# Another hand-written order of the same pieces, up to the middle of the first feed-forward layer

## The chip, the cores and the metric

The kernel runs on one core of one Trainium2 chip. The metric is the device time of the core in microseconds (us). It is given as the median of three runs of the kernel before; one further execution was profiled, and all rows below come from that one.

## What is computed

Local attention with block summaries, then two feed-forward layers, all in float32 at the interface (weights of the layers come as float64):

```python
scores_l = scale * (q @ k.T)            # batch 2, 8 heads, 768 positions, head size 64
scores_l = where(|i - j| < 16, scores_l, -1e9)
scores_s = scale * (q @ k_block_max.T) + log(32)     # 24 blocks of 32 keys
a = softmax(concat(scores_l, scores_s))
x = a @ concat(v, v_block_mean)         # heads side by side: 2 x 768 x 512
h = relu(x @ w_in)                      # 512 -> 1024
x = (h * sigmoid(conv3(h, conv_w))) @ w_out          # 1024 -> 512
x = x + relu(layernorm(x) * g_ln @ w_ch1) @ w_ch2    # 512 -> 2048 -> 512
```

## The kernel before

**Pieces and order.** The kernel first describes its work as 1932 pieces (`plan.op`), each with a name, the engines that may do it and what it must follow. The string ORDER lists them: `583V` is piece 583 on VectorE. The letters are P (TensorE), V (VectorE), A (ScalarE), G (GpSimd) and S (SP, which issues nearly all DMAs). `Plan.arrange` reads the list, and `Plan.trace` emits the pieces in that order. Each engine runs its own pieces strictly in the order of the list, and waits at a piece whose inputs or buffers are not ready; nothing behind it on that engine overtakes it.

**Stages.** For each batch the keys, queries and values come in from HBM in chunks; TensorE transposes keys (pieces kt, kb) and queries (qt), lines 374 and 367. Attention then works on units of 128 rows (64 queries of each of two windows, for four heads of one parity); two units make a group of 128 positions. Unit u has a mask product M*u* (line 479), which fills the score bank, a transpose of its probabilities P*u* (line 586) and VectorE's, ScalarE's and GpSimd's softmax between them (lines 545, 557, 565, 576). Group j, with units 2j and 2j+1, has one score product S*j* (line 487) and one value product T*j* (line 503), the **value group** of this text:

```python
for h_ in range(2):
    vv = vw[j % 3][0:NK, h_, :].rearrange("p (h e) -> p h e", h=4)
    for p in range(4):
        for a in range(2):
            T.matmul(av[...], vv[:, p, s_], ps[a][:, p, 64 * h_:64 * h_ + 64], start=True, stop=True)
```

There are 16 matmuls in a value group and 32 in the trace, since a float32 product goes twice. The value tile `vw` (three buffers) has 120 rows: 24 block means and 96 local positions. Its first half `h_ = 0` and its second half are loaded by two DMAs, piece lv*j* (line 621). The block means come once for each buffer and batch, piece vs*j* for j of 0, 1, 2 and 6, 7, 8, on VectorE or as a DMA on SP:

```python
if e == "S":
    nc.sync.dma_start(out=t[0:NB], in_=src)       # L634
else:
    on[e].tensor_copy(t[0:NB], src)               # L636
wt = [VSUM[b]] + old
LVS[i] = plan.op(f"vs{i}", (("S", 60), ("V", 602)), f_vs, wt, dma=273)
```

T*j* waits for lv*j*, vs*j* (j modulo 3) and the evacuated probabilities of both its units.

**First feed-forward layer.** Forty hidden steps h0 to h39 (three parts a, b, c of four matmuls, line 741) and their output products x (line 818), with relu, convolution, gate and splitting on the other engines. The weights w_in and w_out come as float64 and are narrowed in place in staging buffers; their loads are the pieces lw0 to lw15 (lines 681 and 684, 512 KB each). lw6, lw7, lw8 and all later ones wait until the narrowing of an earlier weight has left their buffer; the last step of that is GpSimd's (line 664). crow is a small load (lc1, 2 KB) that TensorE transposes (cc4, line 906) for the convolution's coefficients. Two pieces warm0 and warm are dummy bfloat16 matmuls, 10 and 6 (line 290).

The second layer (lines 1288 and 1366) takes the second half of the time.

Of the kernel before, what the change touches and what calls it, by code (L numbers as in the profile page):

```python
# [3 lines left out]
13S 12S 15S 14S 67S 9S 8G 3G 4G 5G 6G 68V 58V 0V 31P 32A 59A 69A 16S 11S 18S 17S 20S 73S 91S 19S 21S 39P 27P 34P 41V  # L4
33V 70V 60V 29V 24P 40A 28A 25A 71G 7V 72G 184G 30G 163G 35V 36V 50P 42P 26V 44V 10S 79S 85S 103S 22S 23S 52P 51A 65P
167P 190P 166P 209S 53A 38V 74V 43V 46V 47A 75A 76V 189P 168P 66A 93A 92V 169V 77G 37G 170A 191P 176V 177A 78G 171G
109S 63P 1P 54P 64V 199V 94V 48V 172V 178G 173V 80V 192V 200A 81A 174P 193A 45V 179V 201V 180V 202V 82V 203V 234G 95G
61P 216P 217P 218P 194G 83G 195V 196G 84G 181P 204P 55P 226V 105A 87A 219V 182V 62V 175V 86V 56P 227A 205A 220A 164S
115S 187S 57A 210P 197P 240P 239P 241P 214S 228G 104V 229V 88V 89A 211A 111A 198A 230V 215V 221V 165V 222V 110V 242V
231P 183P 2P 212P 249V 406S 243A 97S 250A 223G 244G 224P 188V 112V 106V 245V 251G 90G 116V 246V 232A 185A 247P 117A  # L10
225A 213V 186V 252V 206P 253V 107A 233P 118V 49A 248A 235A 207V 108G 413P 412P 414P 208V 96G 119A 113A 121S 236V 377S
254P 407P 409P 422V 237G 423A 259P 114G 120G 260P 261P 272P 273P 274P 262A 424G 263G 408V 410V 415V 416A 275A 123A 98V
255V 425V 264V 426V 265V 122V 285P 286P 127S 386S 411S 238S 133S 287P 298P 427P 276A 417G 99A 288A 289A 266A 428A 277V
278V 124V 437P 436P 299P 290V 100V 300P 311P 312P 438P 378P 313P 267V 268G 129A 279A 291V 301A 101A 292A 302A 125A
418V 280V 314A 269G 128V 439V 324P 270P 381P 271P 325P 102G 446V 681S 126G 303V 379V 315A 447A 440A 380V 293V 419V
304V 130V 369S 139S 316V 305A 281A 131A 135A 326P 327A 382A 282V 337P 338P 339P 350P 351P 352P 420P 421A 294G 448G
430G 441G 132G 317V 134V 295V 306V 383V 442V 136V 283P 256P 328A 353A 257A 354A 318A 449V 329V 330V 319V 429P 387P
137A 258V 138G 434G 284P 682P 388A 431A 307A 340A 389V 432V 433G 390P 373P 296P 297P 456P 457P 370P 458P 683A 331A
374A 341A 308V 355V 140V 450V 342V 356V 332V 141A 320A 459A 343V 344A 357A 321V 443V 142V 371A 391A 358V 372V 151S
145S 469P 309P 470P 153A 310P 471P 472A 482P 392V 375V 143G 144G 460V 483P 451P 484P 495P 496P 435S 147A 676A 473A  # L20
345V 485A 486A 677A 474V 461V 157S 399S 395S 710S 475V 476A 462V 487V 322P 497P 444P 508P 323P 509P 510P 463A 152V
464V 477V 376V 146V 488V 452A 333A 334V 498A 404A 499A 445A 684P 148V 154V 690P 689P 685A 385V 453P 158V 511A 500V
159A 713P 489A 712P 160V 521P 346A 149A 522P 490V 400V 405A 523P 150G 161A 691P 524A 454A 714P 155A 501V 393S 699V
335P 512A 732S 156G 722V 700A 336P 347V 162G 534P 396V 502A 535P 359A 348P 360G 536P 503V 686G 349P 692V 537A 525G
361P 687S 513V 538A 465G 455V 547P 362A 397S 365P 514V 737S 466V 548P 526V 366A 478G 549P 701V 539V 515A 479G 467P
527V 468P 707G 702V 516V 480P 491A 550A 492V 481P 528A 540V 394V 493P 504A 693A 494P 505G 566P 517G 529V 567P 703V
733P 694V 568P 367V 398V 506P 569A 551A 507P 541A 723A 579P 552V 530G 580P 695V 542V 581P 518V 724G 715V 704P 531G
582A 739P 734A 570V 740P 592P 705A 696V 519P 716A 725V 571V 401V 520P 572V 553V 593P 402A 543G 384V 583A 532P 403S
726G 554A 544V 680A 533P 594P 584V 741P 717V 555V 718V 595A 556G 697P 573A 749V 557G 727P 742V 750A 596G 545P 574V
585V 546P 719V 743A 558P 698V 688S 605P 738S 606P 728A 711S 744G 575G 607P 678G 720P 608A 679G 562P 559A 751G 609G  # L30
586A 735P 576G 761P 610V 706P 736A 563A 587V 760P 721V 618P 759S 588G 752V 619P 745V 753V 762P 597V 904P 770V 620P
598V 577P 621A 611V 560A 771A 622G 631P 708V 589G 632P 709V 633P 599A 772V 578P 600V 763V 754P 634A 601G 612A 905P
623V 729P 764A 773V 746V 624V 906P 774V 625A 730A 747P 907V 755A 590P 602V 908A 731V 644P 635V 645P 626V 591P 765V
613V 914V 646P 614G 766V 636V 603P 647A 748V 775P 767V 604P 776A 637V 915A 657P 627G 658P 659P 768P 660A 778G 628G
926P 638A 756P 769A 639V 561A 909V 910V 927P 777P 757V 911G 758V 928P 779A 615V 916V 917V 912P 929V 616P 648V 930A
780V 617P 649V 781G 629P 650V 661A 640G 936V 630P 651A 931G 662V 937A 782P 564V 663V 932V 783P 641V 933G 913A 784P
796P 785A 642P 786V 652V 797P 653A 664A 654V 798P 938V 939V 787V 810P 799A 788V 811P 800G 665V 789A 812P 924G 940V
643P 813A 925S 824P 814A 666G 903S 667G 815V 655P 656P 790V 941P 918V 791A 825P 801V 792G 668P 802V 826P 669A 838P
816V 827A 363V 803A 672P 828G 942A 839P 670A 829V 817A 364A 804V 934P 840P 830V 673A 805G 818V 852P 841A 831A 853P
# [1422 lines left out]
```

## Time and profile before

| | |
|---|---|
| median of three runs | 473.87 us (473.40 to 473.89) |
| the profiled execution | 473.54 us |
| its span, first to last instruction | 471.8 us |
| TensorE busy | 461.9 us (98%) |
| VectorE busy | 352.2 us (75%) |
| ScalarE busy | 249.4 us (53%) |
| GpSimd busy | 142.1 us (30%) |

Times in the rows count from the first instruction of the span. PE is TensorE, DVE VectorE, ACT ScalarE, POOL GpSimd, SPq the queue of SP that issues DMAs. A row of the timeline stands for several equal instructions; its second number reaches to the modelled end of the last, so it overlaps the next row a little, and what a piece takes is better read from the start of one row to the start of the next. In brackets stands the idle time ahead of the row and what ended it.

### The profile page before, as it was taken

What the parts mean: (1) busy time and instruction counts of PE and PEld (TensorE: products, weight loads), DVE (VectorE), ACT (ScalarE), POOL (GpSimd) and SP (SyncE); (2) the same over time, 40 slices, a digit from 0 to 9 for tenths busy, and PEclk for the clock granted to TensorE, in tenths of its full rate; (3) what the DMA queues carried; (4) which work ended last, traced back from release to release, by engine and by line L of the source; (5) the groups of instructions that cost most, each with busy time, mean ns of one, the idle gap of its engine ahead of it and who ended that gap; (6) DMA issues with size and microseconds to landing.
All of it is one profiled execution on the core that took longest, in us unless ns stands there. A gap on an engine that the chain in (4) does not pass through costs nothing.

```text
span 471.8 us, 8644 instructions
## 1 busy us (share of the span) xinstructions
PE 461.9 (98%) x3211; PEld 408.6 (87%) x3211; DVE 352.2 (75%) x705; ACT 249.4 (53%) x654; POOL 142.1 (30%) x185
## 2 busy tenths in 40 slices
PE   5999999999999999999999999999999999999996
PEld 5758999888899989988889899999898898998985
DVE  2899999996777857988998874677655677654643
ACT  2788989676766766968954432232343235322010
POOL 3547432554234244232523222131131332002000
PEclk9999999999999999999999999999999999999999
DMA  8999966902002202002221141202222022110213
GB/s 232 327 251 229 246 203 155 176 3 64 1 18 47 92 2 89 1 0 89 92 86 54 39 134 50 86 16 74 89 90 89 3 89 81 44 54 1 99 36 133
DMA packets 56121, 43.26 MB, mean 92 GB/s; under 512 B 34404, under 2 KB 46976, under 8 KB 56080
## 3 DMA queue, kind: packets, MB, share of 16 engines
q1 hardware_dynamic: 55936, 42.65, 32.4%
q8 instruction: 25, 0.41, 0.4%
q14 instruction: 16, 0.13, 0.1%
q10 hardware_dynamic: 144, 0.07, 0.1%
HBM read 39.22 MB, written 3.15 MB: 90 GB/s over the span
## 4 chain that ended last, share of the span: by engine, by line
PE 92%; DVE 3%; DMA 2%; ACT 2%; issue 1%; SPq 0%; POOL 0%; ACTq 0%; DVEq 0%; POOLq 0%
PE acc L1366 26%; PE ch L1288 22%; PE x L818 12%; PE h L741 6%; PE tr L741 5%; PE ch L741 4%; PE tr L487 2%; PE tr L503 2%; PE h L818 2%; PE tr L586 2%; PE tr L367 1%; PE tr L479 1%; PE tr L374 1%; PE x L881 1%; PE x L374 1%; DMA early<-in_k_dram 1%
## 5 line engine op out<-in xcount | busy, mean ns | idle before, releaser
L1366 PE MATMUL acc<-w,cb 128*128 128x512 f32 x570 | 138.1, 390 | 0.0
L1366 PEld LDWEIGHTS acc<-w,cb 128*128 128x128 f32 x570 | 106.4, 188 | 18.4
L1288 PE MATMUL ch<-xb,w 128*128 128x384 f32 x384 | 75.6, 338 | 0.3 <-DVE u L1299 0.3
L1288 PEld LDWEIGHTS ch<-xb,w 128*128 128x128 f32 x384 | 67.8, 188 | 3.2 <-DVE u L1299 1.0
L1299 DVE TENSOR_TENSOR u<-ch,u 128x384 f32<-128x384 f32 x64 | 34.9, 552 | 30.5 <-PE ch L1288 29.8
L1288 PE MATMUL ch<-xt,w 128*128 128x384 f32 x288 | 57.0, 338 | 0.3 <-DVE u L1299 0.2
L771 DVE SCALAR_TENSOR_TENSOR c<-h,ccol,c 128x256 f32<-128x256 f32 (+1 forms) x80 | 48.4, 615 | 9.3 <-POOL c L269 4.9
L1288 PEld LDWEIGHTS ch<-xt,w 128*128 128x128 f32 x288 | 50.8, 188 | 2.8 <-DVE u L1299 1.1
L818 PE MATMUL x<-wo,ghi 128*128 128x512 f32 x160 | 51.1, 401 | 0.0
L1099 POOL TENSOR_TENSOR w<-raw,w 128x512 fp32r<-128x512 f32 (+1 forms) x16 | 20.5, 1283 | 81.9 <-ACT w L1166 75.0
L1308 ACT ACTIVATE cb<-p 128x384 fp32r<-128x384 f32 x32 | 16.5, 519 | 40.4 <-PE acc L1366 23.6
L557 ACT ACTIVATE prob<-tr,nm 128x120 f32<-128x120 f32 x96 | 33.2, 368 | 5.6 <-DVE nm L545 3.6
L647 ACT ACTIVATE raw<-raw 128x512 f32<-128x512 f32 x32 | 21.0, 672 | 26.8 <-DMA raw<-in_moe_w_ch_dram 26.8
L741 PE MATMUL h<-xT,wi 128*128 128x258 f32 x216 | 32.0, 289 | 0.0
L818 PE MATMUL x<-wo,glo 128*128 128x512 f32 x80 | 31.6, 395 | 0.0
L818 PEld LDWEIGHTS x<-wo,ghi 128*128 128x128 f32 x160 | 27.9, 189 | 3.3 <-ACT wo L265 0.2
L1308 ACT ACTIVATE cb<-u 128x384 fp32r<-128x384 f32 x32 | 16.1, 521 | 27.4 <-DVE u L1299 27.3
L741 PEld LDWEIGHTS h<-xT,wi 128*128 128x128 f32 x216 | 29.1, 190 | 1.7 <-ACT h L753 0.2
L741 PE MATMUL tr<-xT,wi 128*128 128x386 f32 (+1 forms) x168 | 29.3, 317 | 0.0
L741 PEld LDWEIGHTS tr<-xT,wi 128*128 128x128 f32 x168 | 26.7, 190 | 1.3 <-issue 0.4
L652 DVE SCALAR_TENSOR_TENSOR raw<-raw 128x512 uint32<-128x512 uint32 x32 | 22.9, 727 | 0.7 <-ACT raw L647 0.2
L786 DVE SCALAR_TENSOR_TENSOR gbuf<-c,h 128x256 f32<-128x256 f32 (+1 forms) x40 | 19.3, 487 | 5.2 <-ACT c L776 5.1
(192 smaller groups left out, 830.0 us busy)
## 6 DMA issues: line engine op xcount, KB each, us to landing
raw<-in_moe_w_ch_dram SPq DMA_DIRECT2D x32, 512.0 KB, 3.6
wst<-in_moe_w_out_dram SPq DMA_DIRECT2D x8, 512.0 KB, 4.8
vw<-in_v_dram SPq DMA_DIRECT2D x20, 192.0 KB, 4.6
wst<-in_moe_w_in_dram SPq DMA_DIRECT2D x5, 512.0 KB, 8.3
s_q<-in_q_dram SPq DMA_DIRECT2D x8, 256.0 KB
early<-in_k_dram SPq DMA_DIRECT2D x6, 256.0 KB, 5.0
x2a<-in_moe_w_in_dram SPq DMA_DIRECT2D x3, 512.0 KB
early<-in_v_dram SPq DMA_DIRECT2D x3, 512.0 KB
```

The source lines that it names most:

```text
L557: A.activation(out=pr[:, p, :], in_=sc[:, p * NK:(p + 1) * NK], func=AF.Exp, bias=nm[:, p:p + 1], scale=1.0, accum_out=sm[:, p:p + 1])
L647: A.activation(out=f, in_=f, func=AF.Prelu, scale=F64_SCALE, alpha=F64_SIGN)
L652: V.scalar_tensor_tensor(out=most, in0=most, scalar=3, in1=least, op0=ALU.logical_shift_left, op1=ALU.bitwise_or)
L741: T.matmul(live["h", i][:, 0:N + 2], w_[:, c, f * 128:(f + 1) * 128], x_[:, c, 0:N + 2], start=(k_ == 0 and c == 0), stop=(k_ == 2 and c = ...
L771: V.scalar_tensor_tensor(out=ct, in0=ht[:, kk:kk + N], scalar=ccol[:, kk * NF + f:kk * NF + f + 1], in1=ct, op0=ALU.mult, op1=ALU.add)
L786: V.scalar_tensor_tensor(out=gt, in0=ct, scalar=1.0, in1=ht, op0=ALU.add, op1=ALU.mult)
L818: T.matmul(x2ps[g, t], l[:, ts_], r[:, f, :], start=(f == 0 and j == 0), stop=(f == NF - 1 and j == 2))
L1099: lambda e: on[e].tensor_tensor(out=hi()[1], in0=from_(), in1=hi()[0].bitcast(F32), op=ALU.subtract),
L1288: T.matmul(bk[k], l[:, c, :], x_[:, c, :], start=j == 0 and c == 0, stop=j == 2 and c == 1)
L1299: lambda e: V.tensor_tensor(out=temp(to), in0=bk[k], in1=temp(x), op=ALU.add), after,
L1308: A.activation(out=half(0, r, y), in_=temp(src), func=AF.Relu)
L1366: T.matmul(acc[key], ct_[n][l][:, r, 128 * t:128 * t + 128], w2[s][k][:, r], start=first and j == 0, stop=done and j == 5)
```

## The change

Only ORDER is another list. It has the same 1932 pieces. The first 757 of them stand in another order, up to the last pieces ahead of hidden step h24 (24 of 40); the remaining 1175 are the same in the same order. 88 pieces change their engine: 21 from VectorE to GpSimd, 17 from GpSimd to VectorE, 15 from VectorE to ScalarE, 13 from ScalarE to VectorE, 13 from GpSimd to ScalarE, 5 from ScalarE to GpSimd, 3 from VectorE to SP and one from SP to VectorE. The first lines of the two lists:

```diff
-13S 12S 15S 14S 67S 9S 8G 3G 4G 5G 6G 68V 58V 0V 31P 32A 59A 69A 16S 11S 18S 17S 20S 73S 91S 19S 21S 39P 27P 34P 41V
...
+5G 7G 184G 3G 12S 27P 29V 28A 15S 39P 41V 40A 14S 34P 13S 16S 67S 6G 68V 69A 36V 35A 70V 11S 31P 42P 24P 20S 163G 44V 33V 0V 26V 18S 52P 43A 17S 50P 32V
...
```

The new list is broken into longer lines, so that every line of the code behind it has a number smaller by 24.

**SP's queue around the first value loads.** wst and x2a are staging for weights, vw_99, vw_100 and vw_101 the three value tiles, vsum the block means, crow the small load. Before:

```order
L954 DMA s_q<-in_q_dram 128x8x64 x2
L681 DMA wst<-in_moe_w_in_dram 128x4x256
L621 DMA vw_99<-in_v_dram 80x8x64
L621 DMA vw_99<-in_v_dram 96x8x64
L684 DMA wst<-in_moe_w_out_dram 128x1024
L621 DMA vw_100<-in_v_dram 96x8x64 x2
L621 DMA vw_101<-in_v_dram 96x8x64 x2
L954 DMA s_q<-in_q_dram 128x8x64 x2
```

Now:

```order
L930 DMA s_q<-in_q_dram 128x8x64 x2
L657 DMA wst<-in_moe_w_in_dram 128x4x256
L597 DMA vw_99<-in_v_dram 80x8x64
L597 DMA vw_99<-in_v_dram 96x8x64
L597 DMA vw_100<-in_v_dram 96x8x64 x2
L597 DMA vw_101<-in_v_dram 96x8x64 x2
L610 DMA vw_99<-vsum 24x2x512
L610 DMA vw_100<-vsum 24x2x512
L660 DMA wst<-in_moe_w_out_dram 128x1024
L828 DMA crow<-in_moe_g_ln_dram 4x128
L610 DMA vw_101<-vsum 24x2x512
L660 DMA wst<-in_moe_w_out_dram 128x1024
```

The three copies of the block means (vs0, vs1, vs2), which were VectorE's at line 636, now stand on SP behind the value loads, and the weight load lw8 has moved behind the first two of them.

**TensorE around the first value groups.** Before, T0 stands alone ahead of the six warming matmuls, and T1 and T2 stand together behind P4 and P6:

```order
L487 MATMUL tr<-kw_95,qb_98 64x120 x16
L586 MATMUL tr<-ident,prob 120x128 x4
L503 MATMUL tr<-probT,vw_99 64x64 x16
L290 LDWEIGHTS warm
...
L367 MATMUL tr<-ident,s_q 128x128 x4
L586 MATMUL tr<-ident,prob 120x128 x8
L503 MATMUL tr<-probT,vw_100 64x64 x16
L503 MATMUL tr<-probT,vw_101 64x64 x16
L479 LDWEIGHTS mask_l
```

Now:

```order
L343 MATMUL tr<-ident,s_q 128x128 x8
...
L463 MATMUL tr<-kw_95,qb_98 64x120 x16
L562 MATMUL tr<-ident,prob 120x128 x12
L266 LDWEIGHTS warm
...
L479 MATMUL tr<-probT,vw_99 64x64 x16
L479 MATMUL tr<-probT,vw_100 64x64 x16
L455 LDWEIGHTS mask_l
...
L479 MATMUL tr<-probT,vw_101 64x64 x16
L463 MATMUL tr<-kw_96,qb_97 64x120 x16
```

T0 has moved behind P4 and the warming matmuls, to T1; T2 stands alone behind two masks. Further on, T6 and T7, and T8 and T9, which stood alone, stand side by side too; T3 T4 and T10 T11 were pairs and stay pairs. Before, T1 T2, T3 T4 and T10 T11 were pairs; now T0 T1, T3 T4, T6 T7, T8 T9 and T10 T11.

## Rows read from the trace of the kernel before

**Rows 1.** The page: the span, busy time of each engine, the chain by engine.
```profile
span 471.8 us, 8644 instructions
...
PE 461.9 (98%) x3211; PEld 408.6 (87%) x3211; DVE 352.2 (75%) x705; ACT 249.4 (53%) x654; POOL 142.1 (30%) x185
...
PE 92%; DVE 3%; DMA 2%; ACT 2%; issue 1%; SPq 0%; POOL 0%; ACTq 0%; DVEq 0%; POOLq 0%
```
**Rows 2.** Windows: busy time of each engine, TensorE's granted clock, DMA share, GB/s.
```profile
30.00:35.00 5.00, 5.00 (x64) 2.89 (x64) 4.86 (x13) 4.45 (x15) 1.60 (x3) 1.00 1.08 289
35.00:40.00 5.00, 4.55 (x78) 3.44 (x75) 4.85 (x11) 5.00 (x21) 2.61 (x3) 1.00 1.15 183
40.00:133.00 93.00, 93.00 (x1042) 82.88 (x1038) 84.36 (x181) 72.69 (x243) 40.96 (x62) 1.00 0.55 130
```
**Rows 3.** TensorE's timeline, 0 to 45 us: start, length, line, operation, count, idle before.
```profile
3.98 1.98 PE L374 MATMUL tr<-ident,early 128*64 128x128 f32 x16 [3.98 <-DMA early<-in_k_dram]
6.84 1.98 PE L374 MATMUL tr<-ident,early 128*64 128x128 f32 x16 [0.88 <-DMA early<-in_k_dram]
...
25.28 0.24 PE L906 MATMUL x<-ident,crow 28*128 28x28 f32 x1
25.45 0.58 PE L479 MATMUL tr<-mask_r,mask_l 67*128 67x480 bf16 x2
...
34.57 1.15 PE L503 MATMUL tr<-probT,vw 120*64 120x64 f32 x32
35.66 1.47 PE L290 MATMUL h<-warm 128*128 128x512 bf16 x6
36.96 0.60 PE L367 MATMUL tr<-ident,s_q 128*128 128x128 f32 x4
37.40 0.60 PE L586 MATMUL tr<-ident,prob 128*120 128x128 f32 x4
38.45 0.62 PE L586 MATMUL tr<-ident,prob 128*120 128x128 f32 x4 [0.45 <-DVE prob L576]
39.00 2.21 PE L503 MATMUL tr<-probT,vw 120*64 120x64 f32 x64
41.15 0.58 PE L479 MATMUL tr<-mask_r,mask_l 67*128 67x480 bf16 x2
41.66 1.05 PE L487 MATMUL tr<-kw,qb 64*64 64x120 f32 x32
```
**Rows 4.** SP's timeline, 30 to 36 us and at 65.8 us: DMA issues.
```profile
30.36 0.35 SPq L684 DMA_DIRECT2D wst<-in_moe_w_out_dram  x1
30.75 5.28 SPq L621 DMA_DIRECT2D vw<-in_v_dram  x4
...
65.78 0.34 SPq L684 DMA_DIRECT2D wst<-in_moe_w_out_dram  x1
```
**Rows 5.** DMA view at 30.4 and at 65.8 us: issue, KB, us to landing.
```profile
wst<-in_moe_w_out_dram SPq DMA_DIRECT2D x1, 512.0 KB, 6.0
...
wst<-in_moe_w_out_dram SPq DMA_DIRECT2D x1, 512.0 KB, 3.5
```
**Rows 6.** TensorE's timeline, 60 to 134 us: value groups, hidden steps behind other work.
```profile
61.33 2.09 PE L503 MATMUL tr<-probT,vw 120*64 120x64 f32 x64
63.34 0.66 PE L367 MATMUL tr<-ident,s_k 128*128 128x128 f32 x4
...
79.54 1.10 PE L503 MATMUL tr<-probT,vw 120*64 120x64 f32 x32
...
80.81 1.78 PE L741 MATMUL h<-xT,wi 128*128 128x258 f32 x12
...
98.97 1.60 PE L741 MATMUL h<-xT,wi 128*128 128x258 f32 x12
...
112.87 1.15 PE L503 MATMUL tr<-probT,vw 120*64 120x64 f32 x32
```
**Rows 7.** Groups by line, VectorE, 16 to 45 us: the three copies of block means.
```profile
L636 DVE COPY vw<-vsum 24x1024 f32<-24x1024 f32 x3 | 2.0, 676 | 0.1
```
**Rows 8.** Line 634, the later copies as DMAs (ns), and their size.
```profile
L634 SPq DMA_DIRECT2D vw<-vsum x3: 779/779/779, 108.3 to 109.9; - x3
...
vw<-vsum SPq DMA_DIRECT2D x3, 96.0 KB
```
**Rows 9.** Waits of SP's queue, 16 to 60 us: in total, times, longest.
```profile
SPq L684 <- POOL sm L565: 3.8, 2, 2.9
```

More of the change, by code (lines that the diff above doesn't have):

```diff
@@ L94 @@
[L94 to L95 removed]
+5G 7G 184G 3G 12S 27P 29V 28A 15S 39P 41V 40A 14S 34P 13S 16S 67S 6G 68V 69A 36V 35A 70V 11S 31P 42P 24P 20S 163G 44V 33V 0V 26V 18S 52P 43A 17S 50P 32V
+53V 9S 25A 38V 30V 51A 8G 4G 71G 85S 86V 72G 73S 37G 65P 19S 21S 166P 103S 47A 87A 79S 190P 66A 49A 88V 58V 89A 90G 167P 189P 168P 169V 191P 63P 75A 199V
+176V 64V 45G 91S 170A 171G 74V 172V 22S 173V 1P 46V 23S 174P 217P 200A 201G 54P 202V 203G 204P 209S 48A 177A 178G 192V 59A 193A 104V 179V 180V 181P 76V
@@ new lines @@
+105A 106V 77A 78G 80V 216P 218P 219V 109S 93A 175A 194G 81A 164S 220A 221G 226V 227A 55P 82V 187S 56P 92V 94V 107G 234G 182A 205V 195V 57A 212P 213A 210P
+196V 239P 214S 83A 84G 228V 229V 230V 222V 60V 165S 188S 240P 241P 197P 115S 108G 231P 95A 211A 223V 224P 242V 243A 249V 250A 198V 244V 10S 2P 251G 245V
+110V 246V 111A 252V 183P 206P 96G 232A 413P 185V 412P 253G 112V 215S 225A 207A 208V 113A 233P 235A 414P 186V 236V 117A 422V 423A 116V 114G 247P 254P 118V
+61P 121S 62V 237G 259P 415V 260P 255V 424G 425V 119A 261P 262A 248V 97S 426V 272P 273P 274P 416A 127S 285P 286P 287P 263A 427P 275A 276A 417V 264V 418V
@@ new lines @@
+265V 437P 99A 266A 377S 277V 98V 419V 123A 267V 288A 434G 289A 268A 428A 129A 100V 290V 278V 291V 269V 298P 122V 279A 280V 436P 438P 446V 439V 101A 420P
+299P 300P 292A 311P 312P 313P 301A 314A 315V 421A 120G 270P 102G 133S 406S 302A 281A 293V 128V 316V 324P 124V 325P 130V 271P 303V 326P 337P 447A 448V 282V
+304V 440A 134V 338P 339P 125A 327A 378P 135A 328A 411S 379V 380V 305A 329V 306V 317V 409P 381P 136V 382V 350P 351P 352P 353A 131A 318A 383V 330V 410A 319V
+126G 283P 238S 284P 430G 137A 256P 257A 294G 295V 258V 429P 431A 132G 331A 307A 369S 407P 370P 354G 373P 296P 297P 432V 374V 433V 456P 457P 340A 341A 139S
@@ new lines @@
+342V 140V 332V 355V 441V 141A 320A 408A 356V 458P 469P 470P 442V 371A 449V 471P 138G 482P 459A 460A 308V 343V 344A 483P 142V 345V 357A 358V 484P 143A 372V
+375V 385V 386S 485A 387P 388A 389V 461V 462V 472A 486A 321V 676A 463A 333A 390P 391A 450V 681S 487V 443V 464V 488V 393S 392V 473A 144G 489A 490V 474V 495P
+334V 309P 310P 496P 497P 498A 322P 404A 475V 151S 508P 509P 323P 145S 147A 510P 511A 444P 476A 445A 451P 452A 684P 685A 677A 146V 152V 148V 376G 435S 690P
+499V 477V 500V 521P 522P 523P 682P 524A 512G 149A 157S 150G 689P 453P 501V 513V 691P 153A 158V 525G 712P 683A 502A 503V 399S 159A 699V 534P 535P 536P 537A
@@ new lines @@
+368A 854P 806G 843V 674A 671A 919P 866P 920A 844V 855A 867P 935A 921P 845A 565A 846V 943P 856V 675A 857V 793P 1067V 832V 1068G 922V 868P 923V 880P 869A
+944A 1069V 881P 858V 870G 945V 882P 871V 794P 883A 872V 795P 1073S 884V 873A 1078S 807P 885V 1095A 808P 886V 819A 946P 820V 809P 947P 1074V 1075A 833A 821P
+1076V 1096A 834V 948P 1079V 1080A 822P 887A 823P 859A 860V 960P 847A 874V 1077A 835P 1081V 836P 848V 1082A 888V 837P 949A 1083G 1097P 861A 849P 950A 862G
+961P 951V 1085G 850P 851P 1084G 1089A 962P 1093V 1086G 1098P 963A 952V 974P 1110A 863P 1087A 964V 1090A 975P 1104A 1094G 976P 875A 1088A 864P 977A 1091G
@@ new lines @@
+1099V 988P 978A 876G 1191S 1100V 989P 965V 865P 1101V 877P 1102V 889G 966V 1108A 878P 1092G 1105V 953A 879P 967A 954V 990P 1111A 1185S 890V 1002P 991A 955G
+1103V 1003P 968V 979V 891P 992V 895P 956V 980V 1004P 896A 1192V 1113P 892A 1016P 1106A 1112P 1005A 1107V 1017P 981A 993V 1119A 1018P 1006A 982V 1109V 1030P
+1114A 1019A 899P 994V 1020A 1115V 1031P 969A 1007V 900A 1032P 970G 1008V 1125A 957P 897A 995A 958P 1021V 1009A 996V 959P 1187A 1116V 1044P 1022V 983A 1118V
+1033A 971P 1117V 1121A 984V 1045P 1034A 1010V 1122G 1023A 1046P 1035V 901A 893A 972P 1047A 1193A 973P 1126V 1123A 985P 997G 986P 998V 1124V 987P 1128P
@@ L96 @@
+1911P 1920P 1924P 1921V 1918P 1925V 1926P 1919V 1917V 1930P 1923V 1928P 1927V 1931V 1929V
 """
```

135 lines of the change are left out of this document (44 added, 91 removed).

## The prediction

> **What bounds the kernel now.** I read the page first: TensorE is busy 461.9 of 471.8 us, and the chain that ended last is 92% TensorE [rows 1]. So a new order of the same pieces can win only where TensorE stands still or works longer than it must, and it loses whatever new standing it brings. Then the windows: from 40 to 133 us TensorE is busy 93.00 of 93.00 us, from 35 to 40 us 4.55 of 5.00 [rows 2]. The timeline says where the rest is: 3.98 us before the first transpose, 0.88 us before the second, which waits for a load, and 0.45 us at 38.45 us [rows 3]. In the stretch that the change rewrites, that is all there is to win: 1.3 us beside the start itself. Behind it the same 1175 pieces follow in the same order, with TensorE on the chain, so I let a shift at 133 us reach the end unchanged.
>
> The second thing to see is how near the transfers are. From 30 to 40 us the 16 DMA engines are busy all the time (shares 1.08 and 1.15), but move 289 GB/s in the first half and 183 in the second [rows 2]. The weight load lw8 is issued at 30.36 us [rows 4] and takes 6.0 us to land; the same load out of an empty queue at 65.78 us took 3.5 us [rows 5]. So there is a queue of some 2.5 us, and what is issued behind lw8 lands behind it: first the four value loads of lv1 and lv2. The value groups T1 and T2 start together at 39.00 us and take 2.21 us, T3 and T4 take 2.09 [rows 3, 6]: T1 and T2 were held for about 0.1 us inside. T2's second half, which needs lv2's second load, begins three quarters into the pair, 1.5 us after 39.00, so I take that load's landing as 40.4 us. The kernel before already does its first value groups about as early as the loads allow.
>
> **The change, part by part.**
>
> *The start.* The first transposes now stand in the order of their loads, and TensorE needs the second load, not the third, for the second one. That can give back the 0.88 us [rows 3]. I count it with nothing, because it ends in the wait that follows. Bounds: 0 and 0.9 us less, of use only if that wait is not there.
>
> *The value sums by DMA.* T0, T1 and T2 each need the 24 rows of block means in their value tile. Before, VectorE copied them, three copies of 0.676 us [rows 7]. Now vs0, vs1 and vs2 are DMAs on SP's queue: 96 KB each, 0.779 us to issue [rows 8]. vs0 and vs1 stand behind lv2; vs2 stands behind lw8 and the small load of crow as well. VectorE gains 2.0 us of work, which nothing on the path waits for while T0 waits. In return T0, which was free to go once lv0 had landed, must wait for lv1, lv2 and its copy.
>
> When is T0 free? Against the kernel before, lw8's 512 KB are no longer ahead of lv2. At the two rates of [rows 2] they are worth 1.8 us (289 GB/s) or 2.9 us (183 GB/s). lw8 moved in the first half, so I take 1.8. A copy of 96 KB costs 0.34 to 0.54 us by the same rates; I take 0.4. So T0 is free at 40.4 - 1.8 + 0.4 = **39.0 us**; at the other end, 40.4 - 2.9 + 0.4 = 37.9 us. The rates are those of loads from HBM; a copy within SBUF has no row under load here.
>
> When does TensorE get there? Before, T0 started at 34.57 us. The new list does the same pieces ahead of it, without the transpose of crow (0.17 us, from 25.28 to 25.45 us), and with the second transpose of q (0.44), P4 (0.60) and the six warming matmuls (1.30) [rows 3]: 34.57 - 0.17 + 0.44 + 0.60 + 1.30 = 36.7 us, or 35.9 with the better start. **TensorE stands for 2.3 to 3.1 us** at T0, five times the 0.45 us that goes.
>
> What does that cost? The kernel before, at 39.00 us, had done T0 (1.09, from 34.57 to 35.66 us), P6 (0.55, from 38.45 to 39.00) and the crow transpose (0.17) [rows 3], and everything that the new list has done when it comes to T0. So the new list lies 39.0 + 1.09 + 0.55 + 0.17 - 39.0 = **1.8 us** behind. The old wait of 0.45 us is inside this difference. With T0 free at 37.9 us it is 0.7.
>
> *T2 and its copy.* T1's copy lands 0.4 us behind T0's, under T0's own matmuls. The pair ends at 39.0 + 2.0 (the pair at 61.33 us is over at 63.34) = 41.0 us [rows 6], the two masks ahead of T2 take 0.5 (41.15 to 41.66) [rows 3], so T2 is reached at 41.5 us. Its copy lands at 39.4 + 1.8 (lw8) + 0.4 = 41.6 us. I take **0.1 us**; at 183 GB/s it is 1.3. lw8's issue waits for its staging buffer: SP's waits for GpSimd at lines like this one were up to 2.9 us [rows 9], so this end is open.
>
> *The five pairs.* Before, three pairs of value groups stood side by side (T1 T2, T3 T4, T10 T11) and six stood alone; now five pairs and two alone. A group alone takes 1.10 to 1.15 us, a pair 2.09 [rows 6], so a pair saves 0.11 to 0.21. Two pairs more: **-0.3 us** (bounds -0.2 and -0.4).
>
> That is the row for value groups alone. Other changes of shape cost as well: the same 12 matmuls of a hidden step take 1.78 us behind masks and 1.60 behind output products [rows 6]. I counted 83 changes between kinds of TensorE work in the old stretch and 77 in the new one; six changes at 0.18 us would be 1.1 us instead of 0.3. The Trainium skill (TensorEngine Tiling (Array Packing), Key Properties) says that a change of tiling mode drains TensorE. By that rule every one of the six counts, and the sum below would come out 0.8 us lower; the rows show it for some changes and not for others, so I keep 0.3 and leave 1.1 to the low end.
>
> *The other moves.* 88 pieces change engine, the largest parts 21 from VectorE to GpSimd and 17 the other way. VectorE has 84.36 us of work and GpSimd 40.96 in the 93 us from 40 to 133 [rows 2], so no engine becomes the bound by its sum. A single piece may come late, a GpSimd piece above all. I price this at 0, with up to 1 us for the high end.
>
> **Sum.** 1.8 + 0.1 - 0.3 = +1.6 us on the profiled execution's 473.54 us, so 475.1. The median of the three runs, 473.87, lies 0.33 above that execution: **475.5 us**. A measurement of this kernel can tell about 0.2%, 0.95 us, from no change; the forecast lies beyond that.
>
> **Rivals.**
>
> *The copies come early.* If the copies do not wait for the loads ahead of them, T0 finds its rows when TensorE arrives at 35.9 us. Then the 0.88 us and the 0.45 us are won, and the 0.3 us: 473.87 - 1.6 = 472.3 us. For it: only 96 KB each, and an empty queue gives a load back in 3.5 us. Against it: lw8's 6.0 us [rows 5], and the program order of SP, in which the value loads stand first. The Trainium skill (DMA: Bandwidth & Descriptors, Queues, rings and completion order) says that each DMA engine takes its descriptors in ring order and that a semaphore's increment lands behind all earlier writes of that engine; by that rule the copy cannot pass the value loads. This ends on the other side; it decides as soon as T0 is free before about 36.5 us. Chance 0.10.
>
> *The wait is mostly covered.* If the loads run ahead of the rate I took and T0 is free at about 37.5 us, the new list lies 0.3 us behind and the pairs give that back: 473.9 us, no change that can be measured. For it: the second half's 183 GB/s holds many packets of 256 B, which partly leave with the new order. Against: those are the value loads themselves. Chance 0.20.
>
> *The queue runs later still.* lw7 waits for a weight buffer that GpSimd frees, lw8 for another; if either comes 2 us late, every transfer behind it, the copies among them, comes 2 us late, and T2 waits 1.3 us: up to 478.7 us. Also here, new waits for GpSimd between 45 and 133 us. Chance 0.12.
>
> *The order does not do what it says.* The pairs do stand side by side on TensorE in the built order, so I give this no chance.
>
> **How the numbers follow.** The forecast, 475.5, has a chance of 0.58, all slower; with the late queue, slower has 0.70. No change has 0.20, faster 0.10. The range goes from 474.0 us (T0 free at 37.9 us, and half of the 1.1 us for changes of shape) to 477.6 us (T2's 1.3 us and 0.8 us of late pieces on top); faster runs and the worst of the late queue stay outside, 2 in 10.
>
> **What would show it.** Right: in the profile after, a gap on TensorE of 2 to 3 us ahead of a value group at 38 to 40 us, ended by a DMA into vw; warming matmuls that end near 36 us; full TensorE windows from 45 us to 133 us; and the last line's chain behind 135 us shifted by one amount. Wrong: no gap ahead of T0, or a gap that something else ends; new gaps of over 0.5 us behind 45 us; or a first score product well ahead of 17 us whose gain survives to 60 us.

## Result, and the profile after

The changed kernel takes 476.13 us (median of 7 executions, 474.57 to 477.86), the kernel before 473.84 us in the same comparison (7 executions, 473.11 to 475.17). The ratio is 1.0053, with a 95% interval from 1.0033 to 1.0072: **slower by about half a per cent**, as forecast (475.5, from 474.0 to 477.6). The profiled execution took 475.98 us, its span is 474.3 us.

The page's head and chain line, to be read against [rows 1]: TensorE is as busy as before, VectorE 6.5 us less, and the chain is TensorE's again.

```profile
span 474.3 us, 8637 instructions
...
PE 462.2 (97%) x3211; PEld 409.0 (86%) x3211; DVE 345.7 (73%) x697; ACT 253.4 (53%) x664; POOL 142.6 (30%) x181
...
PE 92%; DMA 2%; ACT 2%; DVE 1%; SPq 1%; issue 1%; POOL 0%; ACTq 0%
```

The windows of the changed kernel (columns as in [rows 2]: TensorE, weight loads, VectorE, ScalarE, GpSimd, granted clock, DMA share, GB/s):

```profile
35.00:40.00 5.00, 2.56 (x49) 1.86 (x49) 2.17 (x7) 3.11 (x16) 3.51 (x4) 0.94 1.00 232
40.00:45.00 5.00, 5.00 (x96) 3.87 (x94) 2.99 (x6) 2.98 (x6) 1.31 (x1) 0.72 0.58 187
...
50.00:133.00 83.00, 83.00 (x835) 73.49 (x833) 73.05 (x163) 66.22 (x220) 34.43 (x47) 1.00 0.53 119
```

TensorE is busy 2.56 us of the five from 35 to 40 us, where it was 4.55 [rows 2], and in the next five it is busy throughout at a mean granted clock of 0.72. From 50 us on it is full at clock 1.00. TensorE's timeline shows both:

```profile
5.56 1.95 PE L350 MATMUL tr<-ident,early 128*64 128x128 f32 x16
...
12.68 1.09 PE L350 MATMUL x<-ident,early 128*64 128x128 f32 x16 [0.80 <-DMA early<-in_q_dram]
...
19.57 0.76 PE L350 MATMUL tr<-ident,early 128*64 128x128 f32 x9 [0.52 <-issue]
...
34.52 1.46 PE L266 MATMUL h<-warm 128*128 128x512 bf16 x6
38.42 2.92 PE L479 MATMUL tr<-probT,vw 120*64 120x64 f32 x64 [2.44 <-DVE sm L545]
41.27 0.98 PE L455 MATMUL tr<-mask_r,mask_l 67*128 67x480 bf16 x2
42.18 1.41 PE L479 MATMUL tr<-probT,vw 120*64 120x64 f32 x32
43.52 1.05 PE L463 MATMUL tr<-kw,qb 64*64 64x120 f32 x32
```

Against [rows 3]: the gap of 0.88 us ahead of the second transpose is gone, gaps of 0.80 and 0.52 us have come at 12.68 and 19.57 us, and TensorE stands for 2.44 us ahead of the pair T0 T1. Then that pair takes 2.9 us, where a pair took 2.0, two masks take 0.9 where they took 0.5, and T2 takes 1.3 where a group took 1.1: the granted clock is 0.50 (1.2 of 2.4 GHz) from 39.37 us for 3.41 us, and 1.00 on both sides of that.

The row names a VectorE reciprocal (sm, L545) as what ended the gap. That one was done at 37.70 us, 0.72 us before T0. The trace's DMA records show T0's copy of block means landing at 38.33 us, 0.09 us before T0. SP's timeline shows why so late: all six value loads were issued ahead of the copies, and the weight load lw8, which stood ahead of four of them [rows 4], behind two copies.

```profile
27.54 0.37 SPq L657 DMA_DIRECT2D wst<-in_moe_w_in_dram  x1
27.95 5.45 SPq L597 DMA_DIRECT2D vw<-in_v_dram  x6
33.50 1.77 SPq L610 DMA_DIRECT2D vw<-vsum  x2
35.38 0.45 SPq L660 DMA_DIRECT2D wst<-in_moe_w_out_dram  x1
```

**Where the 2.4 us come from.** The first piece behind the rewritten stretch, P20, starts at 136.20 us, before at 133.08: 3.12 us later. From the starts of the 206 TensorE pieces that both traces show before it, and the idle time in front of them: idle time 3.80 against 1.33 us, +2.47; the first matmul at 3.83 against 3.98 us, -0.15; the first transposes, which ran at half clock until 12.32 us before and until 8.65 us now, -1.04; T0 to T2 and the masks between them at half clock, +1.36; all other pieces together, +0.49. The sum is 3.13. Behind P20 the shift stays 3.1 us up to 360 us and then falls to 2.34: the profiled execution of the kernel before lost 0.8 us between 367 and 391 us, mostly on slow matmuls, with one gap of 0.25 us at 390.86. None of the other profiles told of here shows that loss; whether other executions of the kernel before have it is not shown, since only one was profiled.

### The profile page after: what moved, and what is told of

Read it like the earlier page. It is cut to its first block, busy times and chain, and to the rows that moved or that the text cites. A ratio compares the mean times of both kernels' runs of the same rounds, so it can differ in the third digit from the quotient of the medians.

```text
span 474.3 us, 8637 instructions
## 1 busy us (share of the span) xinstructions
PE 462.2 (97%) x3211; PEld 409.0 (86%) x3211; DVE 345.7 (73%) x697; ACT 253.4 (53%) x664; POOL 142.6 (30%) x181
## 4 chain that ended last, share of the span: by engine, by line
PE 92%; DMA 2%; ACT 2%; DVE 1%; SPq 1%; issue 1%; POOL 0%; ACTq 0%
PE acc L1342 26%; PE ch L1264 23%; PE x L794 12%; PE h L717 6%; PE tr L717 5%; PE ch L717 4%; PE tr L479 3%; PE tr L463 2%; PE tr L562 2%; PE h L794 2%; PE tr L455 1%; PE tr L343 1%; DMA early<-in_q_dram 1%; PE x L857 1%; SPq L323 1%
## 5 line engine op out<-in xcount | busy, mean ns | idle before, releaser
L628 DVE SCALAR_TENSOR_TENSOR raw<-raw 128x512 uint32<-128x512 uint32 x32 | 21.8, 694 | 0.9 <-ACT raw L623 0.5
```

The source lines that it names most:

```text
L628: V.scalar_tensor_tensor(out=most, in0=most, scalar=3, in1=least, op0=ALU.logical_shift_left, op1=ALU.bitwise_or)
```

## Experiments

Each is compared with executions of the kernel before on the same chip (medians 473.2 to 473.4 us). In the lists, 165, 188 and 215 are vs0, vs1 and vs2; 214 is lv2, 2 is warm, 183 is T0. Where a list shows a piece at a new place alone, its old place, not shown, is empty. A landing is the last entry of a transfer in the DMA records; a transfer has 12 or 16 of them, and its reader needs the last.

**1. The copies back on VectorE, in place.**

```diff
-230V 222V 60V 165S 188S 240P 241P
+230V 222V 60V 165V 188V 240P 241P
...
-412P 253G 112V 215S 225A
+412P 253G 112V 215V 225A
```

> The changed list with one part undone: vs0, vs1 and vs2 are VectorE copies again, at the places in the list where the DMAs stood. Theory A (the loss is the wait of T0 for its copy behind the value loads, and the half clock that follows it): no gap of over 1.3 us ahead of T0, T0 at 36 to 37.3 us in place of 38.42, the granted clock stays at 1.00 behind 13 us, the pair T0 T1 takes 2.0 us in place of 2.9; up to 2 us of new waits for VectorE, since it gets 2.0 us of copies back; in total 473.5 to 475.0 us, 1 to 2.5 us under the changed kernel. Theory B (the loss lies in the rest of the new order, the copies only stand where TensorE would wait anyway): T0 at 38 us or later with another releaser, total within 0.5 us of the changed kernel's 476.1.

Measured: 478.05 us, ratio 1.0089 (1.0068 to 1.0110). The median is 1.9 us above the changed kernel's (the two intervals just overlap), so **neither theory held**. T0 starts at 39.81 us, but the gap is elsewhere: TensorE stands 2.92 us ahead of P4's transpose, for VectorE's normalized probabilities, and another 1.20 us ahead of T2, for ScalarE. The clock falls here too, to 0.50 from 38.72 us for 3.41 us.

```profile
37.45 0.63 PE L565 MATMUL tr<-ident,prob 128*120 128x128 f32 x4 [2.92 <-DVE prob L555]
37.92 1.97 PE L269 MATMUL h<-warm 128*128 128x512 bf16 x6
39.81 3.12 PE L482 MATMUL tr<-probT,vw 120*64 120x64 f32 x64
```

VectorE's and GpSimd's timelines of this run:

```profile
33.27 2.38 DVE L615 COPY vw<-vsum 24x1024 f32<-24x1024 f32 x2
35.57 1.73 DVE L555 TENSOR_TENSOR prob<-prob,sm 128x480 f32<-128x480 f32 x1
37.23 1.20 DVE L524 TENSOR_REDUCE nm<-tr 128x4 f32<-128x480 f32 x2
```

```profile
33.23 3.56 POOL L643 TENSOR_TENSOR wi<-wst,wi 128x512 fp32r<-128x512 f32 x2 [1.97 <-ACT wi L244]
```

The first copy took 0.675 us, the second 1.773; the product behind it took 1.73 us, where the same product takes 0.64 in the changed kernel. Both slow ones end about 0.5 us after one of GpSimd's two steps (35.10 and 36.80 us), and these steps are long themselves, 1.87 and 1.74 us where others of them take 1.30. From these times I take it that the two engines do not run these together: one waits for the other, and its record counts the wait as its own length. The Trainium skill (SBUF — State Buffer, Who interferes with whom) says that a VectorE operation in a two-port mode, or with two inputs in SBUF while GpSimd's reads SBUF, and a GpSimd operation lock each other out of a shared pair of ports for a whole instruction. The trace agrees: the copy and the product are held, while the reductions from PSUM in the changed kernel take the usual 0.6 us each beside the same GpSimd steps.

**2. More dummy matmuls instead of standing.**

```diff
-    for nm, n in (("warm0", 10), ("warm", 6)):
+    for nm, n in (("warm0", 10), ("warm", 17)):
```

> The changed list, but piece warm issues 17 dummy matmuls in place of 6: 11 more of 0.22 us fill the 2.4 us for which TensorE stands ahead of T0; nothing else differs. It tells the wait from the clock. Theory A (the half clock behind 39.37 us comes from TensorE standing still just before): T0 still at 38.4 us, without a gap of over 0.3 us, granted clock 1.00 throughout behind 13 us, the pair T0 T1 in 2.0 us, hidden step h0 1.3 to 1.7 us earlier than 45.69 us, total 474.3 to 475.0 us. Rival (the clock falls for another reason, or its fall costs nothing on the path): the clock falls to 0.5 for 3.4 us all the same, or the total stays within 0.5 us of 476.1.

Measured: 475.75 us, 1.0048 (1.0030 to 1.0067). The clock stayed at 1.00 in the profile, and the mean clock was 0.998 or more in 5 of 6 executions. But T0's copy landed at 39.40 us in this execution, so T0 started 1.06 us later than in the changed kernel's profile, behind a gap of 0.65 us (at most 0.3 was expected):

```profile
39.48 2.08 PE L482 MATMUL tr<-probT,vw 120*64 120x64 f32 x64 [0.65 <-issue]
```

Even so h0 started at 45.51 us, 0.18 us earlier. From T0's start to h0 the half clock was thus worth 1.06 + 0.18 = 1.24 us in that pair of traces. In the medians a gain of 0.2 us is within the intervals: as a total the run is inconclusive.

**3. One part alone, in the kernel before.**

```diff
-230V 215V 221V 165V 222V 110V
+230V 215V 221V 222V 110V
...
-240P 239P 241P 214S 228G
+240P 239P 241P 214S 165S 228G
```

> The kernel before with one part of the change alone: vs0 is a DMA on SP's queue right behind lv2; the rest of the list is that of before, lw8 ahead of lv1 and lv2 included. Theory A (a copy on SP's queue lands behind every load issued ahead of it): it lands at 40.5 to 41.5 us, T0 moves from 34.57 to about 41 us, TensorE stands for 5 to 6.5 us in one gap ended by that DMA, the granted clock falls to 0.5 afterwards, total 478.5 to 481 us. Rival C (the small copy of 96 KB does not wait for the loads ahead of it and costs its own 0.4 to 1 us): it lands about 35 to 36 us, T0 at 36 us or earlier, total at most 475.3 us.

Measured: 480.12 us, 1.0136 (1.0114 to 1.0158). Theory A holds; the copy landed at 39.76 us, 0.7 us before the lower end, behind lv2's last load at 39.47 us. TensorE's timeline:

```profile
34.20 0.65 PE L565 MATMUL tr<-ident,prob 128*120 128x128 f32 x4
39.89 1.98 PE L482 MATMUL tr<-probT,vw 120*64 120x64 f32 x32 [5.04 <-DMA vw<-vsum]
41.80 2.10 PE L269 MATMUL h<-warm 128*128 128x512 bf16 x6
```

A group alone takes 1.98 us here instead of 1.10: again 0.50 of the clock, from 39.71 us for 3.41 us. One copy of 96 KB, moved to the queue, costs 6.8 us (480.12 against 473.36).

**4. Two copies on ScalarE's DMA queue.**

```diff
-            if e == "S":
-                nc.sync.dma_start(out=t[0:NB], in_=src)
+            if e in "SA":
+                (nc.sync if e == "S" else nc.scalar).dma_start(out=t[0:NB], in_=src)
...
-230V 222V 60V 165S 188S 240P 241P
+230V 222V 60V 165A 188A 240P 241P
```

> The changed list, but vs0 and vs1 are issued on ScalarE's DMA queue in place of SP's, at the same places of the list; vs2 stays on SP. It tells the copying from the place in the queue. Theory A (the order of SP's queue is what holds the copies): they land 1 to 2 us after they are issued, whatever SP has ahead; issued at 33 to 35 us, T0 at 36 to 37 us, gap ahead of T0 under 1 us, no fall of the clock, total 473.8 to 475.2 us. Rival D (the 16 DMA engines are full, and any copy issued there waits for the same bytes, in whatever queue): landing at 38 us or later, gap of 2 us or more, total 475.8 us or more.

Measured: 476.07 us, 1.0051 (1.0031 to 1.0071). The total is rival D's, the landings are neither theory's in full, and there is a cost of its own. ScalarE's timeline has the two issues:

```profile
32.00 1.42 ACTq L613 DMA_DIRECT2D vw<-vsum  x1
...
33.46 0.80 ACTq L613 DMA_DIRECT2D vw<-vsum  x1
```

TensorE's timeline has the gaps that followed:

```profile
35.50 0.65 PE L565 MATMUL tr<-ident,prob 128*120 128x128 f32 x4 [1.11 <-ACT qb L244]
...
37.38 1.15 PE L482 MATMUL tr<-probT,vw 120*64 120x64 f32 x32
39.67 1.15 PE L482 MATMUL tr<-probT,vw 120*64 120x64 f32 x32 [1.14 <-DMA vw<-vsum]
```

T0 found its copy without waiting at 37.38 us: it had landed at 36.69 us, 3.3 us after its issue was over. T1's landed at 39.53 us, 5.3 us after its issue, although lv1 had landed at 36.16 us. Both copies missed theory A's 1 to 2 us; rival D's 38 us holds for the second alone. The first landed ahead of lv2's two loads (37.78 and 38.89 us), which were issued beside it on SP's queue, the second behind them. SP's queue kept the DMA engines filled meanwhile: the DMA view's lines for SP's queue (q1) and the copies' queue (q10) (packets, MB, share of the engines' time) from 34 to 35 us, then q10's from 38 to 39 us:

```profile
q1 hardware_dynamic: 511, 0.13, 89.4%
q10 hardware_dynamic: 38, 0.07, 37.3%
```
```profile
q10 hardware_dynamic: 8, 0.01, 7.2%
```

The loads had most of the engines' time, and the second copy was still moving at 38 us. The two issues held ScalarE for 2.2 us in all, its evacuation qb came 1.5 us later than in the changed kernel (34.85 against 33.33 us), and that is what P4 waited for.

**5. All three copies ahead on SP's queue.**

```diff
-196V 239P 214S 83A 84G
+196V 239P 165S 188S 214S 215S 83A 84G
```

> The changed list with three DMAs moved on SP's queue and nothing else: vs0 and vs1 ahead of lv2's two loads, vs2 right behind them, ahead of lw8 and crow's load. Theory A (the copies land in the order of SP's queue, so their place in it sets T0): vs0 lands 1.6 to 2.2 us earlier than 38.33, at 36.1 to 37 us; the gap ahead of T0 is 0.3 to 1.3 us in place of 2.44; the granted clock stays at 1.00 behind 13 us; T2 waits 0 to 1 us; total 2 to 3.5 us under the changed kernel, that is within 1 us of the kernel before on either side. Rival D (the DMA engines are full and a copy lands at 38 us wherever it stands): gap of 2 us or more, total within 0.7 us of the changed kernel (1.0053 of before).

Measured: 473.36 us (12 executions, 472.55 to 473.84), 0.9997 (0.9985 to 1.0010). **Theory A holds: the loss is gone from the total.** vs0 landed at 36.88 us.

```profile
34.91 1.46 PE L269 MATMUL h<-warm 128*128 128x512 bf16 x6
36.98 2.08 PE L482 MATMUL tr<-probT,vw 120*64 120x64 f32 x64 [0.60 <-DVE sm L548]
38.99 0.58 PE L458 MATMUL tr<-mask_r,mask_l 67*128 67x480 bf16 x2
40.11 1.15 PE L482 MATMUL tr<-probT,vw 120*64 120x64 f32 x32 [0.54 <-DMA vw<-vsum]
```

In TensorE's timeline above the gap ahead of T0 is 0.60 us, the pair takes its 2.0 us, the clock was 0.998 or more in all 12 executions, and their spread is 1.3 us where the changed kernel's was 3.3. T0 starts 1.44 us earlier than in the changed kernel's profile, h0 2.33 us (43.36 against 45.69). P20 starts at 133.89 us, still 0.81 us behind the kernel before; the two spans are equal (471.8 us) because the profiled execution of before lost its 0.8 us later.

**6. Only two of them ahead.**

```diff
-196V 239P 214S 83A 84G
+196V 239P 165S 188S 214S 83A 84G
```

> As the run with all three copies moved, but vs2 stays where the change puts it, behind lw8 and crow's load. It tells the wait of T2 from that of T0. Theory A: T0 at 36.3 to 37.3 us as there; then T2, reached 2.5 us after T0, stands for 1.3 to 2.2 us until vs2 lands at 41 to 42 us, so that hidden step h0 begins within 0.6 us of where it does in the changed kernel at full clock (44.1 to 45 us) and the total is 474.0 to 475.3 us: most of what T0 wins is given back at T2. Rival (T2 is held by nothing but its place): no gap of over 0.5 us ahead of T2, total as with all three moved.

Measured: 477.61 us (474.89 to 479.72), 1.0089 (1.0059 to 1.0120). Theory A's mechanism holds, its size does not. T0 started at 37.29 us, then TensorE's timeline shows T2 waiting:

```profile
39.31 0.58 PE L458 MATMUL tr<-mask_r,mask_l 67*128 67x480 bf16 x2
43.64 1.98 PE L482 MATMUL tr<-probT,vw 120*64 120x64 f32 x32 [3.75 <-DMA vw<-vsum]
45.55 1.68 PE L466 MATMUL tr<-kw,qb 64*64 64x120 f32 x28
```

vs2 landed at 43.55 us in this execution and at 41.11 in the changed kernel's. TensorE stood 3.75 us, and the clock was 0.50 for 6.83 us from 42.42 us on, before the gap was over. In this profile what T0 won was more than given back at T2. But it is the longest execution of the six: eleven of vs2's twelve entries were there by 42.44 us and the last came 1.11 us later, as in the loads around it. The median, 477.61 us, is 1.5 us above the changed kernel's, within the intervals.

**7. Copies early on VectorE.**

```diff
-196V 239P 214S 83A 84G
+196V 239P 165V 188V 214S 215S 83A 84G
...
-211A 223V 224P 242V
+211A 223V 2P 224P 242V
```

> The changed list with vs0 and vs1 on VectorE again, but early, right behind the first softmax step that follows the block means (near 31.9 us, before GpSimd's two narrowing steps that begin at 33 us); piece warm moves ahead of P4; vs2 stays on SP, right behind lv2. The run with the copies on VectorE at their late place had them at 0.68 and 1.77 us and the next product at 1.73, each ending about 0.5 us after a GpSimd step. If that is a collision of the two engines, the copies now take 0.68 us each, P4 is ready at 35.3 to 36 us, T0 starts at 36 to 37.4 us, the clock stays at 1.00, total 473.0 to 474.6 us. If VectorE's copies are slow wherever they stand, or the collision only moves to another operation, P4 is ready at 37 us or later and the total is 475.5 us or more.

Measured: 476.12 us, 1.0056 (1.0035 to 1.0076). The copies themselves took 0.68 and 0.67 us, as in [rows 7], so VectorE's copies are not slow wherever they stand. But the collision moved on, as VectorE's timeline shows:

```profile
31.37 1.28 DVE L615 COPY vw<-vsum 24x1024 f32<-24x1024 f32 x2 [0.29 <-ACT vsum L244]
32.58 1.26 DVE L544 TENSOR_SCALAR sm<-sm 128x4 f32<-128x4 f32 x1
33.87 0.18 DVE L548 RECIPROCAL sm<-sm 128x4 f32<-128x4 f32 x1
34.09 1.50 DVE L555 TENSOR_TENSOR prob<-prob,sm 128x480 f32<-128x480 f32 x1
```

A four-column operation of 0.15 us takes 1.26, a product of 0.64 takes 1.50, with GpSimd's steps at 32.48 to 35.06 us. TensorE stands 2.41 us ahead of the probability transposes, and the clock falls again, so the second alternative holds:

```profile
35.73 0.62 PE L565 MATMUL tr<-ident,prob 128*120 128x128 f32 x4 [2.41 <-DVE prob L555]
```

At neither of the two places tried, run 1's and this one, does VectorE have room for the two copies ahead of T0; other places were not tried.

**8. The two new pairs taken apart.**

```diff
-729P 904P
+904P 729P
...
-927P 731V 910V 625A 626V 756P
+756P 927P 731V 910V 625A 626V
```

> The changed list with the two new pairs of the later stretch taken apart: a mask product stands between T6 and T7, another between T8 and T9. It measures what a pair is worth. By the rows of value groups (alone 1.10 to 1.15 us, a pair 2.09) the two lose 0.1 to 0.2 us each, 0.2 to 0.4 together; with a price for every change of shape of TensorE's work it would be up to 0.4 each. TensorE's occupancy in the profile between 115 and 140 us tells, since the total can not: 0 to +0.8 us against the changed kernel.

Here 729 is T7, 904 and 927 are masks, 756 is T8. Measured: 477.01 us (4 executions), 1.0080 (1.0051 to 1.0109). TensorE's timeline has T6 and T7 as a pair in the changed kernel,

```profile
119.77 2.08 PE L479 MATMUL tr<-probT,vw 120*64 120x64 f32 x64
```

and apart in this run:

```profile
120.56 1.15 PE L482 MATMUL tr<-probT,vw 120*64 120x64 f32 x32
121.64 0.38 PE L458 MATMUL tr<-mask_r,mask_l 67*128 67x480 bf16 x1
122.38 1.15 PE L482 MATMUL tr<-probT,vw 120*64 120x64 f32 x32 [0.36 <-ACT probT L244]
```

The total says nothing of the pairs, since T0 was late (its copy landed at 39.23 us here). Between T3 and P20 the run loses 0.79 us against the changed kernel (64.38 to 136.20 us there, 65.18 to 137.79 us here): 0.40 us of longer occupancy, most of it on the masks between them, and the gap of 0.36 us ahead of T7, for ScalarE's evacuation.

**9. One dummy matmul instead of six, with the copies ahead.**

```diff
-    for nm, n in (("warm0", 10), ("warm", 6)):
+    for nm, n in (("warm0", 10), ("warm", 1)):
```

The list is run 5's.

> The run with all three copies ahead on SP's queue, but piece warm issues 1 dummy matmul in place of 6. Nothing that T0 waits for changes: its copy lands at 36.9 us as there. TensorE comes to T0 1.1 us earlier and stands 1.6 to 2 us in place of 0.60. It tells what standing costs beyond the wait itself. Theory A (the granted clock falls to half when TensorE has stood, and the half clock costs 1.2 to 1.5 us more): the clock shows 0.5 for 3.4 us behind T0's start in most executions, T0 T1 takes 2.6 to 3 us, total 1.0 to 1.5 us above the run with copies ahead, 1.002 to 1.003 of the kernel before; runs fall into two groups by their mean clock. Rival (standing costs only the wait, or 2 us are too short for the clock to fall): clock 1.00, total as with the copies ahead, 0.9997 of before within 0.0015.

Measured: 473.95 us (12 executions), 1.0014 (1.0004 to 1.0024). T0's copy lands at 36.95 us, 0.07 us from run 5, yet TensorE's timeline reads:

```profile
37.04 2.61 PE L482 MATMUL tr<-probT,vw 120*64 120x64 f32 x64 [2.29 <-DVE prob L555]
39.58 0.98 PE L458 MATMUL tr<-mask_r,mask_l 67*128 67x480 bf16 x2
40.49 1.73 PE L482 MATMUL tr<-probT,vw 120*64 120x64 f32 x32
```

The clock is 0.50 from 38.38 us for 3.41 us and h0 starts at 44.32 us, 0.96 us later than in run 5, although TensorE was given less to do and T2 waits for nothing here (0.54 us in run 5). Of the 12 executions five had a mean clock of 0.995 or 0.996 (median 474.66 us) and seven 0.998 or more (median 473.62). Theory A's mechanism is shown: T0's wait ends at the same time in both runs, and only the standing ahead of it differs. Its size in the total was put too high (0.6 us between the medians, 0.8 by the two ratios), since the clock fell in fewer than half.

**10. vs2 on VectorE, with the other two ahead.** Against run 5's list:

```diff
-165S 188S 214S 215S 83A
+165S 188S 214S 83A
...
-246V 111A 252V 183P
+246V 111A 252V 215V 183P
```

> The run with all three copies ahead, but vs2 is a VectorE copy right ahead of T0's place in the list, where VectorE stands idle from 37.7 us until T0's output comes; vs0 and vs1 stay on SP ahead of lv2. T2 then waits for lv2 alone. Theory A: no or at most 0.3 us gap ahead of T2 (0.54 there), everything behind 0.2 to 0.5 us earlier, total 472.8 to 473.3 us, 0.9985 to 0.9995 of before. Rival (VectorE's copy meets GpSimd's narrowing step of 37.6 to 38.9 us and ends 0.5 us behind it, or holds up VectorE's next work for TensorE): gap ahead of T2 of 0.5 us or more, or a later wait for VectorE, total as with the copies ahead or above.

Measured: 473.21 us (12 executions), 1.0003 (0.9994 to 1.0012). T2 has no gap and starts at 39.42 us, 0.69 us earlier than in run 5, with the copy at 1.80 us beside GpSimd's step. So theory A holds for the gap, and the rival for the total: in the profile P20 starts only 0.13 us earlier, and the total is that of the kernel before. No version was found that beats it.

**11. The changed kernel once more.**

> The changed kernel itself once more, on the same chip as the two runs beside it. Theory A: 1.004 to 1.006 of the kernel before; executions at a mean clock of 1.000 near 474.6 to 475.7 us, those at 0.992 to 0.997 1 to 2 us above them; a gap of 2 to 3 us ahead of T0. Rival (the first measurement was of one chip): a ratio within 0.002 of 1.

Measured: 476.05 us (475.09 to 478.34), 1.0064 (1.0045 to 1.0083). The slowdown repeats. In this profile T0's copy landed at 39.48 us, and TensorE's timeline shows what came of it:

```profile
39.58 3.68 PE L479 MATMUL tr<-probT,vw 120*64 120x64 f32 x64 [3.45 <-issue]
43.19 0.98 PE L455 MATMUL tr<-mask_r,mask_l 67*128 67x480 bf16 x2
44.10 1.88 PE L479 MATMUL tr<-probT,vw 120*64 120x64 f32 x32
```

A gap of 3.45 us, over the expected 3, and a clock of 0.50 for 6.83 us: that execution is the longest of the 13, 478.34 us. Four of the 13 had a mean clock of 1.000 (474.57 to 476.15 us), the other nine 0.992 to 0.996 (475.94 to 478.34).

**The copy and T0, side by side.** Landing by the DMA records, and the first matmul of T0, in nine profiles:

```
run                          vs0 lands   T0 starts
changed kernel                  38.33      38.42
the same again                  39.48      39.58
2  17 dummy matmuls             39.40      39.48
8  pairs taken apart            39.23      39.32
3  before, vs0 on SP            39.76      39.89
5  three copies ahead           36.88      36.98
6  two ahead                    37.20      37.29
9  one dummy matmul             36.95      37.04
10 vs2 on VectorE               36.79      36.88
```

T0 follows its copy by about 0.1 us each time, whatever engine the page names. The copy usually lands behind the load ahead of it in the queue, but not always: in run 8 it landed 0.32 us before the last entry of lv2 (39.55 us).

## Why the prediction was right

**The wait at T0: right in place, cause and size, with two terms off that partly cancel.** T0 free at 39.0 us: 38.42 and 39.58 us in two executions. lv2's last load landed at 40.49 us before (taken as 40.4) and at 37.45 and 38.55 us in those two, so lw8's move was worth 3.0 and 1.9 us (taken as 1.8); the copy landed 0.9 us behind lv2 both times (taken as 0.4). TensorE there at 35.9 us with the better start: 38.42 - 2.44 = 35.98 us. Standing for 2.3 to 3.1 us: 2.44 and 3.45. Run 3 shows it with one copy alone, run 5 takes it away by three places in a queue. The Trainium skill (DMA: Bandwidth & Descriptors, Queues, rings and completion order), cited for it, agrees with these runs: vs0 landed behind lv2's 37.45 us in the changed kernel, and 1.45 us sooner once it stood ahead of it. Run 8's 0.32 us the other way is no contradiction, since the rule is one for each DMA engine by itself, but "cannot pass the value loads" was too strong for the transfer as a whole.

**What standing costs: the step that failed.** "What does that cost?" counted only the standing: 1.8 us by T0's start. In the profile the new list lies 1.2 us behind at T0 (38.42 instead of 39.0 in the same sum). From there to P20 it loses another 1.9 us, where the prediction had +0.1 for T2 and -0.3 for the pairs: 1.36 of it is the half clock behind the gap, which no step has, and the rest lies in other pieces (below). From T0's start to h0 it costs 1.24 us net by run 2 and 0.90 by run 9; T2's gaps of 0.17 and 0.54 us, which only the partners at full clock have, make that 1.4 both times. That the total came out only 0.6 us above the forecast is in part luck: in the two profiles a T0 0.6 us early and the 0.8 us that before's profile lost behind 360 us stand against the missing terms.

**The start, counted at nothing: right.** S3, the last score product ahead of P4 and the warming matmuls, came 0.84 us earlier and the gain ended in T0's wait. That the clock rises at 8.65 us and not at 12.32 (1.04 us) was not foreseen, and ended there too.

**T2's copy: 0.1 us, and no gap was seen,** but by luck: at half clock TensorE reached T2 at 42.18 us, 1.07 us after vs2. With T0 early the wait shows: 3.75 us in run 6, well over the 1.3 us taken as the end, 1.1 us of it for one late entry of that execution.

**The pairs: 0.3 us, right for the value groups.** At full clock (run 5 against before) the ten groups took 0.28 us less. Run 8 gives 0.40 us of occupancy for two pairs, beside a wait. The further 0.8 us, for fewer changes between kinds of work, did not come. In the same comparison masks took 0.50 and query transposes 0.65 us more, output products 0.55 and probability transposes 0.29 us less, and all pieces but the first transposes together 0.43 us more, not less. The Trainium skill's rule that a change of tiling mode drains TensorE (TensorEngine Tiling (Array Packing), Key Properties) was taken to give 0.8 us less; the runs here do not show that. The count behind it was of kinds of work and not of shapes: by the active rows and columns that each matmul's row shows (120*64, 128*120 and so on), the traces change 76 times up to P20 in the kernel before and 76 times in the changed one. So the six fewer changes are no test of the rule. Which neighbours cost what was not tried.

**VectorE's copies: the price was right, the reason wrong.** Moving them off VectorE was counted as 2.0 us that nobody waits for. Runs 1 and 7 show that in this list somebody does: left on VectorE at the places tried, vs0 and vs1 cost as much as on the queue or more, through GpSimd's narrowing steps. Run 10's vs2, where VectorE stands idle, costs nothing.

**The rivals.** What "The copies come early" forecast was brought about by run 5, and gave 473.36 us, not 472.3: T0 still stands 0.60 and T2 0.54 us, and the other pieces keep their 0.4 us. "The queue runs later still" happened in single executions (39.48 us, 478.34 us). Of the signs named, the gap, the end of the warming matmuls and the full windows came true; the shift was one amount up to 360 us only, since the profiled execution of before lost time there.

What stays open: why T0's copy lands 1.15 us apart in two executions of one kernel (0.70 us of it is there when its issue ends, at 34.44 and 35.14 us), and what a better order of masks and transposes would give.

## What to carry to other kernels

A small copy that moves from an engine to a busy DMA queue can cost not its own bytes but the loads issued ahead of it (6.8 us in run 3); look at what stands in the queue, and try another place there before another engine. A gap on TensorE may have to be paid twice, once standing and once at half clock behind it (about 1.4 us each time here), so price it by what it does to the clock of the pieces that follow. Before giving VectorE work, look at what GpSimd does in the same microseconds, and read an unusually long VectorE row as a possible wait.

## What the hardware showed that was not expected

- The granted clock fell from 1.00 to 0.50 in every profile with a gap of 2.29 us or more behind 13 us (2.29 in run 9, 2.41 in run 7, 2.44 in the changed kernel, 2.92 in run 1, 3.10 to 5.04 in others) and stayed there for 3.41 or 6.83 us. In the four with the shorter gaps it fell 0.95 to 1.34 us after TensorE was busy again, in the others before the gap was over. With gaps of 0.60 and 0.54 us (run 5), and of 1.11 and 1.14 us (run 4), it stayed at 1.00. By the mean clock, the same kernel shows both outcomes from one execution to the next.
- A VectorE copy of 0.67 us takes 1.77 or 1.80 beside GpSimd's narrowing step, and a four-column operation of 0.15 us takes 1.26.
- Two copies of 96 KB on ScalarE's DMA queue, beside loads on SP's, took 3.3 and 5.3 us from the end of their issue to their landing (run 4); on SP's queue, in the changed kernel, the same two took 3.9 and 3.6 us.
